# Turning the weights of the states' reads on VectorE and by transfers inside SBUF, turning all states first and all reads last, and splitting the last stores

## The chip, the cores and the metric

The kernel runs on one core of a Trainium2 chip. The metric is the device time of one execution in microseconds (us). Every kernel below was run several times, beside runs of the kernel before on the same chip, and each run comes with the mean clock that TensorE was granted.

The engines are TensorE (PE in the profile; PEld is its weight load), VectorE (DVE), ScalarE (ACT), GpSimd (POOL) and SyncE (SP). SyncE here only issues transfers.

## The reference

Eight batches of eight heads hold 512 tokens and 32 states of width 64. Tokens attend to states, and states attend to tokens. The two results stand below one another (4352 rows of 512) and go through a feed-forward of width 2048.

```python
scores  = x @ state^T / 8;   xread = softmax(scores)  @ state     # 512 rows a batch
scores2 = state @ x^T / 8;   sread = softmax(scores2) @ x         # 32 rows a batch
X = concat(xread, sread) as (8 * 544, 512)
h = X @ w_in                                                      # 512 -> 2048
g = h * erf(max(h, 0) + log1p(exp(-|h|)))
out = g @ w_out                                                   # 2048 -> 512
```

## The kernel before

The token rows of a batch never form `xread`. Their hidden layer is `softmax(scores) @ (state @ w_in)`. The product `state @ w_in` is called the mixing (tile `m`, operands `w_in,st`). It is made of small matmuls of 64 rows by 32 columns, which run side by side on TensorE. The large products (hidden: tiles `h<-`; second products: tiles `o<-`) are done on 2x2 blocks with seven products in place of eight; VectorE makes the sums that this needs. A batch has four groups of hidden and second products. While batch b is in these, the attention of batch b+1 is made beside them.

The parts that the change touches are these:

```python
def states(b):                               # once a batch
    ps = ps_at.tile([P, P], F32, name="at")
    nc.tensor.transpose(out=ps, in_=st[:, b, :], identity=ident)
    stT[b] = keep.tile([P, P], F32, name="stT")
    nc.scalar.copy(stT[b], ps)

def turn_weights(a2):                        # eight transposes, two copies a batch
    a2T = att.tile([P, 2, NC, P], F32, name="sc")
    for e in range(2):
        ps = ps_at.tile([P, NC, P], F32, name="at")
        for c in range(NC):
            nc.tensor.transpose(out=ps[:, c, :], in_=a2[:, e, P * c:P * c + P],
                                identity=ident)
        nc.scalar.copy(a2T[:, e], ps)
    return a2T

def attention(b):
    # [...] turns xq, scores, softmax of both sides
    for e in range(2):
        normalise(both[:, e].rearrange("p (k n) -> p k n", n=Ns))
        nc.vector.transpose(out=aT[b][:, e], in_=both[:, e])
    yield
    a2T = turn_weights(both[:, 2:4])
    yield
    sn = read_tokens(b, a2T, z2)             # 64 small matmuls, sread of one batch
    if b + 1 < B:
        load_x(b + 1)
    yield
    turn_read(b, sn)                         # one transpose and one copy a batch
    yield
```

The argument also rests on the second products and on the sums that they need. The sums are made on VectorE while the first of the products run on TensorE:

```python
def project7(gT, hs, g, first, last, acc):
    # [...]
    for n, (lhs, rhs, bank, c) in enumerate((
            (A12, B21, 0, 0), (A11, B11, 2, 0), (A22, T[4], 1, 0), (S2, T[2], 0, 1),
            (S3, T[3], 2, 1), (S1, T[1], 1, 1), (S4, B22, 3, 0))):
        for i in range(GF):
            if i == 2 and n == 1:
                tt(S1, A21, A22, op=ALU.add)
                tt(S2, S1, A11, op=ALU.subtract)
                tt(S3, A11, A21, op=ALU.subtract)
                tt(S4, A12, S2, op=ALU.subtract)
            nc.tensor.matmul(out=acc[bank][:, E2 * c:E2 * c + E2], lhsT=lhs[:, i, :],
                             rhs=rhs[:, g, i, :], ...)

def put_s(r, ot, c=slice(0, d_model)):       # the last stores, of the states' rows
    m = P // Ns
    rows = out.rearrange("(b t) e -> b t e", t=TB)[m * r:m * r + m, S:]
    nc.sync.dma_start(out=rows[:, :, c], in_=ot[:, c])
```

Of the kernel before, what the change touches and what calls it, by code (L numbers as in the profile page):

```python
# [16 lines left out]
def kernel(  # L17
# [128 lines left out]
    def warm(n):  # L146

        for _ in range(n):
            nc.tensor.matmul(out=spare[:, 0:P], lhsT=ident, rhs=ident, start=True, stop=True)


    sT = const.tile([P, NK, B, Ns], F32, name="sT")
    stT = {}
    aT = {}

    def states(b):

        ps = ps_at.tile([P, P], F32, name="at")
        nc.tensor.transpose(out=ps, in_=st[:, b, :], identity=ident)
        stT[b] = keep.tile([P, P], F32, name="stT")  # L160
        nc.scalar.copy(stT[b], ps)

    over = lambda t: t.unsqueeze(2).to_broadcast([P, NC * NI, Ns])

# [2 lines left out]
    def scores(b, xT):  # L167


        s2 = [ps_at.tile([P, S], F32, name="at") for _ in range(2)]  # L170
        for i in range(NI):
            for e in range(2):
                r, q = slice(D * e, D * e + D), slice(Ns * i, Ns * i + Ns)
                on_pe = nc.tensor.matmul(out=s2[e][q, :], lhsT=stT[b][r, q], rhs=xT[r, i, :],
                                         start=True, stop=True)
        sc = att.tile([P, 2, S], F32, name="sc")
        for e in range(2):
            last = nc.scalar.copy(sc[:, e], s2[e])
        marks[:] = last, on_pe
        return sc, last  # L180
# [21 lines left out]
    def turn_weights(a2):  # L202
# [6 lines left out]
            nc.scalar.copy(a2T[:, e], ps)  # L209
        return a2T  # L210

    def read_tokens(b, a2T, z2):


        xt = x_t.pop(b)
        sr = ps_at.tile([P, 2, D], F32, name="at")
        for e in range(2):
            for c in range(NC):
                for i in range(NI):
                    q = slice(Ns * i, Ns * i + Ns)  # L220
                    nc.tensor.matmul(out=sr[q, e, :], lhsT=a2T[:, e, c, q],  # L221
                                     rhs=xt[:, c, 2 * i + e, :],
                                     start=(c == 0), stop=(c == NC - 1))
        sn = small.tile([P, 2, D], F32, name="sn")
        for e in range(2):
            nc.vector.tensor_scalar(sn[:, e], sr[:, e], z2[:, e:e + 1], None, op0=ALU.mult)
        return sn

    def turn_read(b, sn):
        ps = ps_at.tile([P, NI, Ns], F32, name="at")  # L230
        nc.tensor.transpose(out=ps, in_=sn, identity=ident)
        nc.scalar.copy(sT[:, :, b, :], ps)

    def attention0(between):


        xt = x_t[0]
        xT = att.tile([P, NI, S], F32, name="xT")
        for i in range(NI):
            xp = ps_at.tile([P, S], F32, name="at")  # L240
            for c in range(NC):
                nc.tensor.transpose(out=xp[:, P * c:P * c + P], in_=xt[:, c, 2 * i:2 * i + 2, :],
                                    identity=ident)
            nc.scalar.copy(xT[:, i, :], xp)
        sc, on_act = scores(0, xT)
        both = att.tile([P, NI, S], F32, name="xT")
        a = both[:, 0:2].rearrange("p e (k n) -> p e k n", n=Ns)
        aT[0] = keep.tile([P, 2, S], F32, name="aT")
        for e in range(2):
            s1 = ps_at.tile([P, NC * NI, Ns], F32, name="at")  # L250
            for c in range(NC):
                on_pe = nc.tensor.transpose(out=s1[:, NI * c:NI * c + NI, :],
                                            in_=sc[:, e, P * c:P * c + P], identity=ident)
            m1 = small.tile([P, NC * NI], F32, name="m1")
            nc.vector.reduce_max(out=m1, in_=s1, axis=AX.X)
            on_dve = nc.vector.tensor_tensor(a[:, e], s1, over(m1), op=ALU.subtract)
        between(on_pe, on_act, on_dve)
        for e in range(2):
            on_act = nc.scalar.activation(out=a[:, e], in_=a[:, e], func=ACTF.Exp, scale=scale)
            on_dve = normalise(a[:, e])  # L260
        for e in range(2):
            ps = ps_at.tile([P, S], F32, name="at")
            for c in range(NC):
                nc.tensor.transpose(out=ps[:, P * c:P * c + P],
                                    in_=a[:, e, NI * c:NI * c + NI, :], identity=ident)
            nc.vector.tensor_copy(aT[0][:, e], ps)

        def rest():
            a2 = both[:, 2:4]
            z2 = weigh_tokens(sc, a2)  # L270
            turn_read(0, read_tokens(0, turn_weights(a2), z2))

        return rest, on_act, on_dve

    def attention(b):



        xq = xq_t.pop(b)
        xT = att.tile([P, NI, S], F32, name="xT")  # L280
        turned = nc.vector.transpose(out=xT.rearrange("p i t -> p (i t)"),
                                     in_=xq.rearrange("p i m d -> p (i m d)"))
        if b + 1 < B:
            load_xq(b + 1)
        sc, _ = scores(b, xT)
        marks.append(turned)
        yield
        both = att.tile([P, NI, S], F32, name="xT")
        aT[b] = keep.tile([P, 2, S], F32, name="aT")
        for e in range(2):  # L290
            nc.vector.transpose(out=both[:, e], in_=sc[:, e])
            a = both[:, e].rearrange("p (k n) -> p k n", n=Ns)
            m1 = small.tile([P, NC * NI], F32, name="m1")
            nc.vector.reduce_max(out=m1, in_=a, axis=AX.X)  # L294
            nc.vector.tensor_tensor(a, a, over(m1), op=ALU.subtract)  # L295
            nc.scalar.activation(out=a, in_=a, func=ACTF.Exp, scale=scale)
        z2 = weigh_tokens(sc, both[:, 2:4])
        for e in range(2):
            normalise(both[:, e].rearrange("p (k n) -> p k n", n=Ns))
            nc.vector.transpose(out=aT[b][:, e], in_=both[:, e])  # L300
        yield
        a2T = turn_weights(both[:, 2:4])
        yield
        sn = read_tokens(b, a2T, z2)
        if b + 1 < B:
            load_x(b + 1)
        yield
        turn_read(b, sn)
        yield

    m_t = {}
# [6 lines left out]
    def mixed_part(b, g, j, parts, copy):  # L318
        n = gw // parts
        mg = m_t[b, g][:, :, n * j:n * j + n]  # L320
        fs = slice(2 * g + j, 2 * g + j + 2 // parts)
        ps = [ps_at.tile([P, gw], F32, name="at")[:, 0:n] for _ in range(2)]
        for i in range(NI):
            for e in range(2):
                r, q = slice(D * e, D * e + D), slice(Ns * i, Ns * i + Ns)
                nc.tensor.matmul(out=ps[e][q, :], lhsT=stT[b][r, q],  # L326
                                 rhs=w_in[r, fs, i, :], start=True, stop=True)
        return nc.scalar.copy(mg[:, 0], ps[0]), copy(mg[:, 1], ps[1])

# [200 lines left out]

    def put_s(r, ot, c=slice(0, d_model)):
        m = P // Ns
        rows = out.rearrange("(b t) e -> b t e", t=TB)[m * r:m * r + m, S:]
        nc.sync.dma_start(out=rows[:, :, c], in_=ot[:, c])

    def tiles(n):
        return [ps_o.tile([P, d_model], F32, name="o%d" % r) for r in range(n)]
# [38 lines left out]
            mixed(b, 2 * g + j, copy=copy)  # L576
        combine_m(b, g)

    def begin(on_pe, on_act, on_dve):
        with tc.issue_after(on_pe.ins):  # L580
            warm(32)
        with tc.issue_after(on_act.ins), tc.issue_after(on_dve.ins):
            weights_in(0)

    def behind(marks, f, *args):
        with ExitStack() as order:
            for m in marks:
                order.enter_context(tc.issue_after(m.ins))
            return f(*args)



    warm(10)
    states(0)
    rest, *at = attention0(begin)
    behind(at, weights_in, 1)
    at = mixed(0, 0, 2)
# [7 lines left out]
    for g in range(1, NG):  # L605
# [20 lines left out]
            for j in range(2):  # L626
                behind(at, weights_out, 2 * g + j)
        if g == NG - 1:
            behind(fetched[-1:], load_st)
            behind(fetched[-1:], load_xq, 1)  # L630
            behind(done_, rest)
            load_x(1)
            states(1)
            turn = attention(1)
        gT_, (gT, hs, banks) = gT, hidden(0, range(GF * g, GF * g + GF))
        if g < NG - 1:
# [11 lines left out]
        if g == 2:  # L648
            done(project(gT_, g - 1, acc))
    prepare(1, 1 - begins(1), nc.scalar.copy)  # L650
    done(turn)
    last = behind(at, combine_w)

    def pending():
# [3 lines left out]
    for b in range(1, B + 1):  # L658
# [3 lines left out]
            groups = fast(b, 1, lambda h: put_s)  # L662
        for g, (first, second) in enumerate(groups):
            side = {}
            if b + 1 < B:

                if g == 0:
                    side[4] = lambda: states(b + 1)
                    turn = attention(b + 1)
                    side[6] = lambda: behind(marks, next, turn)  # L670
                elif g == 1:
                    side[0] = side[6] = side[10] = lambda: next(turn)
                else:
                    if g == 2:
                        side[2] = lambda: next(turn)
                    o = g - 2 ^ begins(b + 1)
                    side[4] = lambda: mixed(b + 1, 2 * o)
                    side[8] = lambda: (mixed(b + 1, 2 * o + 1), combine_m(b + 1, o))
                    if g == 3:
                        side[6] = lambda: combine_a(b + 1)  # L680
            elif b + 1 == B and g > 1:

                if g == 2:
# [42 lines left out]
```

## Time and profile before

| | before |
|---|---|
| time, median of 3 runs | 763.88 us (763.88 to 764.07) |
| PE busy | 741.8 us, 97% of the span |
| VectorE busy | 512.7 us, 67% |
| ScalarE busy | 386.8 us, 51% |
| one batch of 2 to 6, start to start | 82.60 us |
| last matmul's start to the end of the span | 8.64 us |

PE is the bound, and a batch is one PE queue with next to no gaps.

### The profile page before, as it was taken

Reading aid. Unit: us, or ns where it says so; the run is one execution under the profiler, and the core shown is the slowest. Engines: PE = TensorE matmul, PEld = TensorE weight load, DVE = VectorE, ACT = ScalarE, POOL = GpSimd, SP = SyncE. Lnnn points to the kernel's source line nnn. Section 1 sums busy time; section 2 is a strip of 40 time slices with the busy share of each in tenths; the row PEclk is TensorE's granted clock in tenths of the full one; section 3 lists DMA queues with packets and bytes.
Section 4 is the critical chain, followed back from the end, with each engine's and each line's share of the span. In section 5 each row is a group of like instructions: output and inputs, shape, how many; then the busy total and the mean of one; then the engine's idle time right before and its main releaser. Section 6 shows DMA issues by size and latency. Waiting matters only on the chain.

```text
span 761.9 us, 12108 instructions
## 1 busy us (share of the span) xinstructions
PE 741.8 (97%) x5076; PEld 595.8 (78%) x5076; DVE 512.7 (67%) x767; ACT 386.8 (51%) x497; POOL 0.7 (0%) x6
## 2 busy tenths in 40 slices
PE   8998999999999999999999999999999999999995
PEld 6533435698888888988888888888898889999994
DVE  3888879856767566947595776756694755684441
ACT  5868864744465544553464446554455344443330
POOL 0000000000000000000000000000000000000000
PEclk9999999999999999999999999999999999999999
DMA  7665752420031201320042003120000000000000
GB/s 225 202 244 202 165 96 70 98 57 28 1 52 43 53 22 17 68 57 28 1 83 57 28 1 51 48 48 22 1 29 2 29 1 28 1 28 1 28 1 29
DMA packets 108587, 42.74 MB, mean 56 GB/s; under 512 B 96116, under 2 KB 99956, under 8 KB 108532
## 3 DMA queue, kind: packets, MB, share of 16 engines
q1 hardware_dynamic: 106420, 41.43, 20.4%
q8 instruction: 40, 0.66, 0.3%
q10 hardware_dynamic: 2112, 0.52, 0.3%
q14 instruction: 15, 0.12, 0.1%
HBM read 33.03 MB, written 8.91 MB: 55 GB/s over the span
## 4 chain that ended last, share of the span: by engine, by line
PE 78%; DVE 10%; ACT 3%; issue 1%; DMA 0%; SPq 0%; DVEq 0%
PE o L503 44%; PE h L397 23%; PE at L326 3%; PE o L453 2%; PE h L439 2%; ACT s L447 1%; DVE hs L405 1%; DVE m L194 1%; PE at L221 1%; DVE z L184 1%; DVE raw L475 1%; DVE xT L295 1%; ACT L447 1%; DVE m L294 1%; DVE s L448 1%
## 5 line engine op out<-in xcount | busy, mean ns | idle before, releaser
L448 DVE TENSOR_TENSOR s<-s,hs 128x2048 f32<-128x2048 f32 x34 | 77.9, 2292 | 74.2 <-ACT s L447 74.1
L404 ACT ACTIVATE s<-hs 128x512 f32<-128x512 f32 x120 | 75.6, 630 | 86.2 <-DVE hs L405 85.9
L503 PE MATMUL o<-w_out,s 128*128 128x256 f32 x480 | 118.3, 380 | 0.0
L503 PE MATMUL o<-raw,hs 128*128 128x256 f32 x480 | 116.3, 385 | 0.0
L503 PE MATMUL o<-w_out,hs 128*128 128x256 f32 x480 | 115.4, 381 | 0.0
L503 PEld LDWEIGHTS o<-raw,hs 128*128 128x128 f32 x480 | 88.4, 190 | 31.4 <-issue 20.1
L503 PEld LDWEIGHTS o<-w_out,hs 128*128 128x128 f32 x480 | 89.8, 190 | 16.3 <-issue 4.2
L405 DVE TENSOR_TENSOR hs<-hs,h 128x512 f32<-128x512 f32 x90 | 61.5, 684 | 49.8 <-PE h L397 49.7
L503 PEld LDWEIGHTS o<-w_out,s 128*128 128x128 f32 x480 | 84.5, 191 | 7.8
L397 PEld LDWEIGHTS h<-aT,m 128*128 128x128 f32 x672 | 84.4, 192 | 6.4 <-issue 1.6
L397 PE MATMUL h<-aT,m 128*128 128x128 f32 x672 | 85.6, 276 | 0.4 <-DVE hs L405 0.4
L405 DVE TENSOR_TENSOR hs<-s,h 128x512 f32<-128x512 f32 x60 | 41.1, 685 | 56.2 <-PE h L397 55.8
L447 ACT ACTIVATE s<-s 128x2048 f32<-128x2048 f32 x34 | 65.0, 1911 | 0.4
L408 ACT COPY s<-h 128x512 f32<-128x512 f32 x30 | 17.5, 582 | 92.4 <-PE h L397 92.4
L453 PE MATMUL o<-w_out,s 128*128 128x512 f32 x128 | 59.1, 600 | 0.9 <-DVE s L448 0.9
L397 PE MATMUL h<-sy,sx 128*128 128x128 f32 x448 | 59.5, 275 | 0.0
L397 PEld LDWEIGHTS h<-sy,sx 128*128 128x128 f32 x448 | 56.7, 192 | 2.2 <-ACT hs L413 0.6
L503 PE MATMUL o<-raw,s 128*128 128x256 f32 x240 | 57.9, 379 | 0.0
L413 ACT COPY hs<-h 128x512 f32<-128x512 f32 x30 | 17.4, 582 | 73.7 <-PE h L397 73.7
L503 PEld LDWEIGHTS o<-raw,s 128*128 128x128 f32 x240 | 43.3, 191 | 4.6
L453 PEld LDWEIGHTS o<-w_out,s 128*128 128x128 f32 x128 | 23.1, 191 | 30.0 <-issue 28.8
L447 ACT ACT_TABLE_LOAD x34 | 43.6, 1283 | 0.6
(112 smaller groups left out, 902.7 us busy)
## 6 DMA issues: line engine op xcount, KB each, us to landing
raw<-in_moe_w_in_dram SPq DMA_DIRECT2D x8, 1024.0 KB, 5.2
raw<-in_moe_w_out_dram SPq DMA_DIRECT2D x8, 1024.0 KB, 4.9
x<-in_x_dram SPq DMA_DIRECT2D x60, 128.0 KB, 2.7
xq<-in_x_dram SPq DMA_DIRECT2D x112, 64.0 KB, 2.1
out_dram<-ot SPq DMA_DIRECT2D x19, 256.0 KB, 2.0
out_dram<-ot SPq DMA_DIRECT2D x30, 128.0 KB, 1.7
x<-in_x_dram ACTq DMA_DIRECT2D x4, 128.0 KB, 4.1
st<-in_state_dram SPq DMA_DIRECT2D x8, 56.0 KB, 4.2
```

What stands on the lines that cost most here:

```text
L184: nc.vector.reduce_sum(out=z1, in_=a, axis=AX.X)
L326: nc.tensor.matmul(out=ps[e][q, :], lhsT=stT[b][r, q], rhs=w_in[r, fs, i, :], start=True, stop=True)
L397: last = nc.tensor.matmul(out=bank[:, q], lhsT=lhsT, rhs=rhs, start=(first and i == 0 and k == 0), stop=(i == GF - 1 and k == len(ops) - 1 ...
L404: nc.scalar.activation(out=s[:, k], in_=hs[:, k], func=ACTF.Softplus)
L405: add = lambda o, x, y: nc.vector.tensor_tensor(o, x, y, op=ALU.add)
L408: nc.scalar.copy(m1, p)
L413: nc.scalar.copy(c11, p)
L439: on_pe = nc.tensor.matmul(out=hp, lhsT=m_t[b, f // GF][:, e, P * (f % GF):P * (f % GF) + P], rhs=aT[b][:, e], start=(e == 0), stop=(e == 1))
L447: return (nc.scalar.activation(out=s, in_=s, func=ACTF.Erf), nc.vector.tensor_tensor(s, s, hs, op=ALU.mult))
L448: nc.vector.tensor_tensor(s, s, hs, op=ALU.mult))
L453: nc.tensor.matmul(out=acc[r], lhsT=gT[:, i, P * r:P * r + P], rhs=w_out[:, GF * g + i, :], start=(g == 0 and i == 0), stop=(g == NG - 1 a ...
L503: nc.tensor.matmul(out=acc[bank][:, E2 * c:E2 * c + E2], lhsT=lhs[:, i, :], rhs=rhs[:, g, i, :], start=(first and i == 0 and c == 0), stop ...
```

## The change

The intent was to take 64 transposes out of PE's queue. VectorE turns the weights in 32x32 blocks, and sixteen transfers from SBUF to SBUF put the blocks in their places. All eight states are turned in the first batch, in place of four of the 32 warm-up matmuls there. All eight reads are turned together in the last batch. The last stores are split as well, so that each goes to one batch's 32 rows and two engines issue them.

```diff
-    def states(b):
+    def states(bs):
+        ps = ps_h.tile([P, len(bs), P], F32, name="h")
+        for k, b in enumerate(bs):
+            last = nc.tensor.transpose(out=ps[:, k], in_=st[:, b, :], identity=ident)
+        nc.scalar.copy(st[:, bs[0]:bs[-1] + 1, :], ps)
# [... cut]
-    def turn_read(b, sn):
+    def turn_read(bs):
+        ps = ps_at.tile([P, len(bs), NI, Ns], F32, name="at")
+        for k, b in enumerate(bs):
+            nc.tensor.transpose(out=ps[:, k], in_=sn_t[b], identity=ident)
# [... cut: attention]
-        a2T = turn_weights(both[:, 2:4])
-        yield
-        sn = read_tokens(b, a2T, z2)
+        nc.vector.transpose(out=both[:, 0:2], in_=both[:, 2:4])
+        a2T = att.tile([P, 2, NC, P], F32, name="sc")
+        blocks = both[:, 0:2].rearrange("p e (c m n) -> p m (e c) n", m=NI, n=Ns)
+        rows = a2T.rearrange("p e c (i n) -> p i (e c) n", n=Ns)
+        for m in range(NI):
+            for i in range(NI):
+                nc.sync.dma_start(out=rows[Ns * m:Ns * m + Ns, i],
+                                  in_=blocks[Ns * i:Ns * i + Ns, m])
+        yield
+        read_tokens(b, a2T, z2)              # now in the batch's own first quarter
# [... cut: put_s]
-        rows = out.rearrange("(b t) e -> b t e", t=TB)[m * r:m * r + m, S:]
-        nc.sync.dma_start(out=rows[:, :, c], in_=ot[:, c])
+        for j in range(m):
+            r0 = TB * (m * r + j) + S
+            queue = nc.scalar if r == 1 or (c.start and j % 2) else nc.sync
+            queue.dma_start(out=out[r0:r0 + Ns, c], in_=ot[Ns * j:Ns * j + Ns, c])
# [... cut: begin]
+        behind(fetched[-1:], load_st)
+        on_pe = behind([on_pe], warm, 12)
+        for bs in range(1, 5), range(5, B):
+            on_pe = behind([on_pe], states, bs)
+        return behind([on_pe], warm, 16)
```

More of the change, by code (lines that the diff above doesn't have):

```diff
@@ L148, in warm @@
         for _ in range(n):
-            nc.tensor.matmul(out=spare[:, 0:P], lhsT=ident, rhs=ident, start=True, stop=True)
+            last = nc.tensor.matmul(out=spare[:, 0:P], lhsT=ident, rhs=ident, start=True,
+                                    stop=True)
+        return last
     sT = const.tile([P, NK, B, Ns], F32, name="sT")
-    stT = {}
     aT = {}
-    def states(b):
-        ps = ps_at.tile([P, P], F32, name="at")
-        nc.tensor.transpose(out=ps, in_=st[:, b, :], identity=ident)
-        stT[b] = keep.tile([P, P], F32, name="stT")
-        nc.scalar.copy(stT[b], ps)
+    def states(bs):
[3 more added lines that the diff above has]
+        nc.scalar.copy(st[:, bs[0]:bs[-1] + 1, :], ps)
+        return last
     over = lambda t: t.unsqueeze(2).to_broadcast([P, NC * NI, Ns])
@@ L173, in scores @@
                 r, q = slice(D * e, D * e + D), slice(Ns * i, Ns * i + Ns)
-                on_pe = nc.tensor.matmul(out=s2[e][q, :], lhsT=stT[b][r, q], rhs=xT[r, i, :],
+                on_pe = nc.tensor.matmul(out=s2[e][q, :], lhsT=st[r, b, q], rhs=xT[r, i, :],
                                          start=True, stop=True)
@@ L210, in turn_weights @@
         return a2T
+    sn_t = {}
     def read_tokens(b, a2T, z2):
@@ L218, in read_tokens @@
             for c in range(NC):
-                for i in range(NI):
+                for i in reversed(range(NI)):
                     q = slice(Ns * i, Ns * i + Ns)
@@ L223, in read_tokens @@
                                      start=(c == 0), stop=(c == NC - 1))
-        sn = small.tile([P, 2, D], F32, name="sn")
+        sn = sn_t[b] = const.tile([P, 2, D], F32, name="sn0") if b == 0 else \
+            st[:, b - 1, :].rearrange("p (e d) -> p e d", e=2)
         for e in range(2):
             nc.vector.tensor_scalar(sn[:, e], sr[:, e], z2[:, e:e + 1], None, op0=ALU.mult)
-        return sn
-    def turn_read(b, sn):
-        ps = ps_at.tile([P, NI, Ns], F32, name="at")
-        nc.tensor.transpose(out=ps, in_=sn, identity=ident)
-        nc.scalar.copy(sT[:, :, b, :], ps)
+    def turn_read(bs):
+        ps = ps_at.tile([P, len(bs), NI, Ns], F32, name="at")
+        for k, b in enumerate(bs):
+            nc.tensor.transpose(out=ps[:, k], in_=sn_t[b], identity=ident)
+        nc.scalar.copy(sT[:, :, bs[0]:bs[-1] + 1, :].rearrange("p i b n -> p b i n"), ps)
     def attention0(between):
@@ L256, in attention0 @@
             on_dve = nc.vector.tensor_tensor(a[:, e], s1, over(m1), op=ALU.subtract)
-        between(on_pe, on_act, on_dve)
+        on_pe = between(on_pe, on_act, on_dve)
         for e in range(2):
@@ L263, in attention0 @@
             for c in range(NC):
-                nc.tensor.transpose(out=ps[:, P * c:P * c + P],
-                                    in_=a[:, e, NI * c:NI * c + NI, :], identity=ident)
+                with tc.issue_after(on_pe.ins):
+                    nc.tensor.transpose(out=ps[:, P * c:P * c + P],
+                                        in_=a[:, e, NI * c:NI * c + NI, :], identity=ident)
             nc.vector.tensor_copy(aT[0][:, e], ps)
@@ L270, in rest @@
             z2 = weigh_tokens(sc, a2)
-            turn_read(0, read_tokens(0, turn_weights(a2), z2))
+            read_tokens(0, turn_weights(a2), z2)
         return rest, on_act, on_dve
@@ L300, in attention @@
             nc.vector.transpose(out=aT[b][:, e], in_=both[:, e])
+        nc.vector.transpose(out=both[:, 0:2], in_=both[:, 2:4])
[6 more added lines that the diff above has]
+                                  in_=blocks[Ns * i:Ns * i + Ns, m])
         yield
-        a2T = turn_weights(both[:, 2:4])
-        yield
-        sn = read_tokens(b, a2T, z2)
+        read_tokens(b, a2T, z2)
         if b + 1 < B:
             load_x(b + 1)
-        yield
-        turn_read(b, sn)
         yield
@@ L325, in mixed_part @@
                 r, q = slice(D * e, D * e + D), slice(Ns * i, Ns * i + Ns)
-                nc.tensor.matmul(out=ps[e][q, :], lhsT=stT[b][r, q],
+                nc.tensor.matmul(out=ps[e][q, :], lhsT=st[r, b, q],
                                  rhs=w_in[r, fs, i, :], start=True, stop=True)
@@ L577, in prepare @@
         combine_m(b, g)
-    def begin(on_pe, on_act, on_dve):
-        with tc.issue_after(on_pe.ins):
-            warm(32)
-        with tc.issue_after(on_act.ins), tc.issue_after(on_dve.ins):
-            weights_in(0)
     def behind(marks, f, *args):
@@ L589, in behind, with begin @@
             return f(*args)
+    def begin(on_pe, on_act, on_dve):
+        behind([on_act, on_dve], weights_in, 0)
+        behind(fetched[-1:], load_st)
[3 more added lines that the diff above has]
+        return behind([on_pe], warm, 16)
     warm(10)
-    states(0)
+    states(range(1))
     rest, *at = attention0(begin)
@@ L628 @@
         if g == NG - 1:
-            behind(fetched[-1:], load_st)
             behind(fetched[-1:], load_xq, 1)
@@ L632 @@
             load_x(1)
-            states(1)
             turn = attention(1)
@@ L650 @@
     prepare(1, 1 - begins(1), nc.scalar.copy)
-    done(turn)
     last = behind(at, combine_w)
@@ L664 @@
             side = {}
+            if b < B and g == 0:
+                side[2] = lambda turn=turn: next(turn)
             if b + 1 < B:
                 if g == 0:
-                    side[4] = lambda: states(b + 1)
                     turn = attention(b + 1)
@@ L671 @@
                 elif g == 1:
-                    side[0] = side[6] = side[10] = lambda: next(turn)
+                    side[0] = lambda: next(turn)
                 else:
-                    if g == 2:
-                        side[2] = lambda: next(turn)
                     o = g - 2 ^ begins(b + 1)
@@ L680 @@
                         side[6] = lambda: combine_a(b + 1)
+            elif b + 1 == B and g == 1:
+                side[4] = lambda: [turn_read(range(k, min(k + 4, B))) for k in range(0, B, 4)]
             elif b + 1 == B and g > 1:
```

## The prediction

> **What bounds the kernel now.** I read the page first, then the stretches of one batch each, then the timeline inside one batch, the waits of the tensor engine, and last the end of the kernel.
>
> ```profile
> PE 741.8 (97%) x5076; PEld 595.8 (78%) x5076; DVE 512.7 (67%) x767; ACT 386.8 (51%) x497; POOL 0.7 (0%) x6
> ...
> PE 78%; DVE 10%; ACT 3%; issue 1%; DMA 0%; SPq 0%; DVEq 0%
> ```
>
> The first line is busy time by engine, the second the engines on the chain that ended last. TensorE is the bound, with VectorE on the chain for a tenth of the span. Batches 1 to 6 are alike:
>
> ```profile
> 225.52:308.12 82.60, 82.40 (x604) 70.06 (x603) 57.12 (x92) 41.61 (x55) 0.00 (x0) 1.00 0.18 41
> 308.12:390.70 82.58, 82.38 (x603) 70.06 (x602) 57.10 (x92) 41.60 (x55) 0.00 (x0) 1.00 0.17 39
> ```
>
> The columns are length, then PE, PEld, DVE, ACT, POOL busy. A batch takes 82.6 us, PE is busy in all but 0.2 of it, VectorE in 57. So PE work taken out of a batch shortens it, if VectorE, which has 25 us to spare on average, is not late where PE needs it. The timeline of PE in the second quarter of a batch, where the attention of the next batch is made:
>
> ```profile
> 236.98 0.60 PE L503 MATMUL o<-raw,s 128*128 128x256 f32 x2
> 237.41 0.38 PE L207 MATMUL at<-ident,xT 128*128 128x128 f32 x2
> 237.63 1.96 PE L503 MATMUL o<-raw,hs 128*128 128x256 f32 x8
> 239.43 0.82 PE L207 MATMUL at<-ident,xT 128*128 128x128 f32 x6
> 240.09 0.38 PE L503 MATMUL o<-w_out,hs 128*128 128x256 f32 x1
> ```
>
> The columns are start and time covered. One transpose is listed at 273 ns, but that is latency. From start to start, six take 240.09 - 239.43 = 0.66 us: 0.11 us each is what one costs the queue. VectorE in the same place:
>
> ```profile
> 235.68 0.70 DVE L300 STREAM_TRANSPOSE aT<-xT 128x512 f32<-128x512 f32 x1
> 236.30 0.65 DVE L405 TENSOR_TENSOR hs<-hs,h 128x512 f32<-128x512 f32 x1
> 236.87 0.67 DVE L500 TENSOR_TENSOR hs<-hs,s 128x512 f32<-128x512 f32 x1
> 237.47 0.68 DVE L501 TENSOR_TENSOR hs<-s 128x512 f32<-128x512 f32 x1
> ```
>
> There is no idle time between these, nor back to about 222.7: here VectorE is full. L500 makes the operand of the PE group that starts at 237.63 and is ready at 237.54. The average of 67% hides that this quarter has 0.1 us of slack. PE already waits once in it:
>
> ```profile
> PE h L397 <- DVE hs L405: 1.4, 6, 0.4
> ```
>
> That is us in total, times, longest: 0.4 us in nearly every batch, the only matmul wait listed between 142 and 630 us. The end:
>
> ```profile
> SPq L721 <- DMA out_dram<-ot: 5.7, 1, 5.7
> ...
> DMA packets 397, 0.53 MB, mean 44 GB/s; under 512 B 12, under 2 KB 268, under 8 KB 396
> ```
>
> The first line: SyncE waits 5.7 us for the last store. The second counts the packets after 750 us: only 12 small ones, the completion writes of three stores, so four engines for each store.
>
> **What the Trainium skill says.** "VectorE: DVE Perf Modes", The three transpose paths: VectorE turns 32x32 blocks only, TensorE a full 128x128 into PSUM. The code before uses both so, and the trace has 0.68 to 0.70 us for 128x512 on VectorE. "TensorE: Matmul & The Clock Gate", Part 4: PE-mode transpose, gives about 275 ns in a kernel, mostly access latency; the trace has 273 listed and 0.11 between starts, which agrees and is why I count 0.11. "DMA: Bandwidth & Descriptors", Why a DMA increments its semaphore by 16 and not by 1: the engines used are the largest number up to 16 that divides the slowest dimension of both sides. The last stores have a slowest dimension of 4 on the DRAM side; 12 completions for three stores agree. The same page, Specifications: under 512 B a transfer is not at line rate. The load of xq, in 128 B packets, shows what that means here: from 219 to 231 us its sixteen transfers of 64 KB moved at about 130 GB/s.
>
> **The change, part by part.**
>
> *Out of each steady batch on PE.* Eight transposes of the weights, one of the states, one of the read: 10 x 0.11 = 1.1 us. The wait for the copy of the turned states before the scores (weight loads at L174 waited 1.8 us in five times) is mostly under other work; the start before it is 0.1 us late. Together 1.2 us in each of six batches: 7.2 us.
>
> *Into VectorE.* One turn of 128x1024. From 0.70 us at 512 columns and 2.30 at 2048 (L281), I estimate 0.70 + 512 x 1.6/1536 = 1.23 us, in seven batches. It overwrites the half that the last L300 reads, so it falls in right after that, in the full stretch, and ahead of L500, as softmax work was issued ahead of L500 all along. L500 then ends at 237.54 + 1.23 = 238.8. PE, without its two transposes, asks at 237.41: a new wait of up to 1.4 us, more than the batch saves. If L500 is put first there is none. I cannot see which from the diff and take half, 0.65 us x 6 = 3.9 us given back. Net for the steady batches: 3.3 us.
>
> *Out of ScalarE.* Two copies of 0.57 us and two of 0.25 in each batch. ScalarE is off the bound at 42 of 82.6 us; nothing counted.
>
> *Transfers.* Sixteen of 32 KB in 128 B packets: 4096 packets a batch, half of xq's. Sixteen xq issues took 9.3 us. The read is moved to the first quarter of the next batch, some 55 us later, so the transfers are hidden. The exception is batch 1: softmax ends near 116 us, issue and landing take until about 125, and PE read the tokens at 121. There PE already stands 1.8 us before L231 at 128.5, as VectorE is late, so most of the wait replaces another.
>
> *The first batch.* Out go two read transposes with waits of 0.4 and 1.8 us, eight weight transposes (0.9) and one state. But from 104 to 129 us the chain is VectorE, which gets 1.23 more and loses 0.47 (the read's scaling moves on). At the start, two copies (about 1.0 us, est. from 0.58 for 512 columns) enter ScalarE where it is full from 12.2 to 17.8 us, and the states' load goes ahead of weights that are not needed before 15.6. The turning itself takes the place of warm-up matmuls: 12 + 7 + 16 for 32. I count 0.5 us gained in all.
>
> *The last batches.* Eight transposes appear in batch 7: 8 x 0.11 = 0.9 us lost.
>
> *The end.* The last add ends at 754.1. Each final store becomes four of 32 rows, so sixteen engines each, on two issuing queues. A 128 KB store on sixteen engines lands in 1.7 us (page, DMA issues). Two issues of some 0.36 us and 1.7 to 2 us of landing give about 756.7 instead of 754.66 + 5.7 = 760.4. I count 3.5 us gained.
>
> Sum: -3.3 - 0.5 + 0.9 - 3.5 = -6.4; 763.9 - 6.4 = 757.5 us.
>
> **The rivals.**
>
> *VectorE gives all of it back.* For it: L500 has 0.1 us of slack and a wait of 1.4 would exceed the 1.2 saved. Against: the order could be luckier, and VectorE loses the read's scaling from the next quarter. Then steady batches stay at 82.6 to 82.8, and the time is 760 to 762 us.
>
> *No wait at all, PE gets all.* For it: average load of VectorE is only 69% in a batch; the turned weights are not needed for 55 us, so a good order would put them behind L500. Then 81.4 us a batch, and 753 to 754 us.
>
> *Transfers become the wait.* If the sixteen small transfers, or the loads of x and the stores behind them on the same queue, are late, PE stands before the read in every batch. Against it: they have some 55 us, and SyncE would be issuing for about a third of a batch (9.3 us for xq, as much for these, some 8 for x and the stores). It would cost several us a batch and make the change slower, 770 or more. I give it 2%.
>
> *The start is delayed by the states' load.* ScalarE and the weights are near the path there; it would cost 1 to 3 us once.
>
> **Range and chances.** The two ends of the VectorE question are 753.6 and 762.0; the first batch and the end add about 1.5 us either way. 752.5 to 763 should hold it 8 times in 10. Two per cent faster is 748.6, which needs the full 7.2, the 3.5 and another 5 us from the first batch: 3%. Two per cent slower needs waits for transfers in all batches: 2%.
>
> **What would show it.** Starts of equal groups a batch apart: 81.4 means the whole PE gain, 82.6 means VectorE took it. A PE wait of L503 for the line of L500 (the sums of the second product) in the second quarter would be the new wait. In the end, 3 x 4 x 16 = 192 instead of 12 completion writes, and SyncE's last wait near 2 us in place of 5.7. Wrong would be: PE waiting for the transfers of the turned weights in steady batches, a first batch longer by over 2 us, or the last wait unchanged.

## More of the kernel before

The order in which an engine receives its instructions is set by the compiler's scheduler, except where the kernel says `issue_after`.

## The result, and the profile after

The changed kernel took 756.48 us (median of 4 runs, 755.29 to 757.16), and the kernel before took 763.95 beside it (763.88 to 764.07). The ratio is 0.99, with a 95% interval of 0.9883 to 0.9918. A ratio here is the mean time of one kernel's fast runs over the mean of the other's fast runs in the same rounds, so it is not quite the ratio of the medians quoted. The change is 7.5 us faster: less than 2%, but clear of noise. The predicted 757.5 was 1 us off.

The page of the changed kernel, busy time by engine and the chain that ended last:

```profile
PE 740.5 (98%) x5012; PEld 590.9 (78%) x5012; DVE 520.8 (69%) x774; ACT 381.1 (51%) x473; POOL 0.7 (0%) x6
...
PE 81%; DVE 8%; ACT 2%; issue 1%
```

PE has 64 instructions fewer, VectorE has 8 us more work, and VectorE's share of the chain has gone down, from 10% to 8%. Two steady batches, with the columns length, PE, PEld, DVE, ACT, POOL busy:

```profile
226.42:307.97 81.55, 81.48 (x594) 68.83 (x594) 58.22 (x93) 40.39 (x51) 0.00 (x0) 1.00 0.21 46
307.97:389.52 81.55, 81.48 (x595) 68.83 (x594) 58.23 (x93) 40.39 (x51) 0.00 (x0) 1.00 0.22 46
```

A batch takes 1.05 us less than before. That is nearly all of the 1.1 us that ten transposes cost PE, so nothing of it was lost to a late VectorE. The timeline of VectorE in the stretch where the prediction expected the trouble:

```profile
237.02 1.23 DVE L310 STREAM_TRANSPOSE xT<-xT 128x1024 f32<-128x1024 f32 x1
238.17 0.65 DVE L512 TENSOR_TENSOR hs<-s 128x512 f32<-128x512 f32 x1
238.74 0.68 DVE L514 TENSOR_TENSOR hs<-s 128x512 f32<-128x512 f32 x1
239.34 0.68 DVE L513 TENSOR_TENSOR hs<-hs,s 128x512 f32<-128x512 f32 x1
```

The turn takes the estimated 1.23 us. It stands where it was expected, ahead of the sums. L512 to L514 make the sums S1, S3 and S2, in this order. S2 (L513) is now ready only at 240.02. Counted from the start of its group's first hidden product that is 13.8 us, where it was 12.0 before (237.54 against 225.52): 1.75 us later, as the turn, S1 and S3 now stand just before it (S1 had been made at 222.66 before). PE in the same stretch:

```profile
236.95 1.46 PE L516 MATMUL o<-raw,s 128*128 128x256 f32 x6
238.25 1.05 PE L410 MATMUL h<-aT,m 128*128 128x128 f32 x8
239.14 0.60 PE L516 MATMUL o<-raw,hs 128*128 128x256 f32 x2
239.57 1.03 PE L516 MATMUL o<-w_out,hs 128*128 128x256 f32 x4
```

PE does not wait. Between the products that need no sum (`raw,s`) and the next ones stand eight products `h<-aT,m`, which belong to the next group. Before, they came after all the second products: the first hidden product of that group stood at 246.65, and now it stands at 238.25. The products on the sums are also in another order. The two `raw,hs` at 239.14 start before S2 is ready, so they can only be on S1 (ready at 238.82), the other sum that meets a `raw` operand. The four `w_out,hs` at 239.57 are by the same reasoning on S3 (ready at 239.42); before, S2 came first. So two things fill the hole, the eight hidden products and the products on the earlier sums. This order is the same in three profiles of the changed kernel, so it is the compiled order. Why the scheduler chose it is not recorded. The waits of PE's matmuls from 142 to 630 us (total, times, longest) are now one line, and the old wait (1.4 us in six times, 0.4 at most) is not among them:

```profile
PE o L516 <- DVE s L461: 0.2, 1, 0.2
```

The SBUF transfers, in the page's list of issues (count, size, median us from issue to landing), and then SyncE's last wait:

```profile
sc<-xT SPq DMA_DIRECT2D x112, 32.0 KB, 1.9
```

```profile
SPq L736 <- DMA out_dram<-ot: 1.6, 1, 1.6
```

No PE wait in a steady batch names the transfers. SyncE's wait for the last store is 1.6 us where it was 5.7. The packets from 742 us to the end, and the issues there:

```profile
DMA packets 576, 0.53 MB, mean 38 GB/s; under 512 B 192, under 2 KB 448, under 8 KB 576
...
out_dram<-ot SPq DMA_DIRECT2D x6, 32.0 KB, 1.6
out_dram<-ot ACTq DMA_DIRECT2D x2, 32.0 KB, 1.6
```

There are 192 small packets where there were 12, so each of the twelve stores uses sixteen engines.

Where the time went can be read from equal places in the two traces. The zero is the first hidden product of batch 0, because the start of the two profiles differs by chance (see the experiments). The changed kernel's column is its third profile, which started as the kernel before did.

| from the first hidden product, us | before | changed | difference |
|---|---|---|---|
| that product, from the span's start | 23.34 | 23.31 | 0.0 |
| batch 1 begins | 92.18 | 91.44 | -0.7 |
| batch 2 begins | 182.48 | 180.88 | -1.6 |
| batch 7 begins | 595.50 | 589.04 | -6.5 |
| states' rows begin | 668.86 | 664.50 | -4.4 |
| last matmul starts | 729.91 | 725.56 | -4.4 |
| span ends | 738.6 | 730.0 | -8.6 |

### The profile page after: what moved, and what is told of

It is laid out like the page before. It is cut to its first block, busy times and chain, and to the rows that moved or that the text cites. A ratio compares the mean times of both kernels' runs of the same rounds, so it can differ in the third digit from the quotient of the medians.

```text
span 754.5 us, 12132 instructions
## 1 busy us (share of the span) xinstructions
PE 740.5 (98%) x5012; PEld 590.9 (78%) x5012; DVE 520.8 (69%) x774; ACT 381.1 (51%) x473; POOL 0.7 (0%) x6
## 4 chain that ended last, share of the span: by engine, by line
PE 81%; DVE 8%; ACT 2%; issue 1%
PE o L516 46%; PE h L410 25%; PE at L339 4%; PE o L466 3%; PE h L452 2%; DVE hs L418 1%; PE at L226 1%; DVE m L197 1%; DVE z L187 1%; PE at L177 1%; DVE raw L488 1%; ACT s L460 1%; DVE xT L303 1%; ACT L460 1%; DVE xT L190 0%
```

## The experiments

My theory was this. Stores and batches each give about half of the gain, and the batches keep PE's whole gain only because the scheduler moved other products into the hole that VectorE's turn makes. The rival was that VectorE was never late, because it had 25 us to spare in each batch. A second question was whether the first batch loses time, at its start (the first profile of the changed kernel had its first hidden product at 24.70, 1.4 us later than before) or at its end, where VectorE is the chain.

### The new stores alone

The kernel before, with one edit:

```diff
-        rows = out.rearrange("(b t) e -> b t e", t=TB)[m * r:m * r + m, S:]
-        nc.sync.dma_start(out=rows[:, :, c], in_=ot[:, c])
+        for j in range(m):
+            r0 = TB * (m * r + j) + S
+            queue = nc.scalar if r == 1 or (c.start and j % 2) else nc.sync
+            queue.dma_start(out=out[r0:r0 + Ns, c], in_=ot[Ns * j:Ns * j + Ns, c])
```

> The kernel before with one part of the change: the last stores cut into blocks of 32 rows on two issuing queues. Theory: from the last matmul's start to the end of the span the kernel before takes 761.9 - 753.3 = 8.6 us and the changed one 754.5 - 750.1 = 4.4 us, and that is the stores alone. So 763.9 - 4.2 = 759.7 us here, with TensorE's last matmul where it was, 192 small completion packets at the end and a last wait of SyncE near 1.6 us. Rival: the gain of 7.5 us is all work taken from TensorE, and the end of the stores is not in the measured time: 763.9 us.

Its three fast runs took 761.41, 760.3 and 760.05 us, and the kernel before 763.93 (median of 7). The ratio is 0.9955 (0.9938 to 0.9971), about 3.4 us. The profiled run was slow (854.01 us at a mean clock of 0.849) and is not compared. That is the 3.5 of the prediction; this run's own expectation, read off the ends of the two profiles, was 4.2. As the profile is slow, the end in this kernel is not compared.

### Everything but the stores

The changed kernel with the old `put_s`, the reverse of the edit above.

> The changed kernel with the old last stores (one transfer for a tile). If the two parts simply add, 756.5 + 4.2 = 760.7 us, and what is left, some 3.2 us against the kernel before, is what moving the transposes earns after all its costs. Rival, the parts share something (the end only became short because TensorE ended in another way): not 760.7 but nearer 756.5.

It took 759.83 us (759.47 to 761.22), a ratio of 0.9948 (0.9933 to 0.9963), or 4.0 us. The two halves add up: 3.4 + 4.0 = 7.4, against 7.5 for the whole change. This rules out that one part covers for the other.

### The weights turned by TensorE again

```diff
# on the changed kernel
-        nc.vector.transpose(out=both[:, 0:2], in_=both[:, 2:4])
-        # [... tile and sixteen transfers]
+        yield
+        a2T = turn_weights(both[:, 2:4])
# [...]
-                    side[0] = lambda: next(turn)
+                    side[0] = side[6] = lambda: next(turn)
```

> The changed kernel, but the weights of the states' reads turned by TensorE again (eight transposes and two ScalarE copies a batch, no VectorE turn, no transfers inside SBUF); states still turned in the first batch, reads turned late, new stores. Theory: each steady batch gets its 8 x 0.11 = 0.87 us back, 81.55 becomes 82.4, and over six batches 5.2 us; the end of the first batch, where VectorE is the chain, gains up to 1.2 us. So 756.5 + 5.2 - 1 = 760.7 us. Rival, VectorE's turn and the transfers cost as much as they save: 756 to 757 us.

It took 759.45 us (758.21 to 761.56), about 3 us more than the changed kernel. In its trace a steady batch takes 82.27 us. Of the 1.05 us that a batch gained, 0.7 is the weights' turning (eight transposes) and 0.3 is the states and reads. At the beginning of batch 2 it is 0.4 us ahead of the changed kernel (180.51 against 180.88), so there VectorE's turn seems to cost more than it saves. The changed kernel's other two profiles have 180.77 and 180.95, so this is little more than the spread.

### The order of PE held as written

On the changed kernel, each second product may only be issued after the one before it, and the next group's first hidden product and the mixing only after the latest second product. No work is added or removed.

```diff
+                with ExitStack() as order:
+                    for m in pe_last:
+                        order.enter_context(tc.issue_after(m.ins))
+                    pe_last[:] = [nc.tensor.matmul(
-                nc.tensor.matmul(
# [... the same issue_after(pe_last) around product(1, p) and around the mixing]
```

> The changed kernel with TensorE's queue held to the program's order where the changed kernel departs from it: the products of the second matmul one behind the other, and the next group's first product and the mixing behind them. VectorE's work is the same. Theory: the compiler put other TensorE work where the late sum of VectorE would have been waited for, and that is why the wait of 1.4 us that I predicted is not there. Held to the order, it is: a wait of L526 for the second product's sums of 1 to 1.5 us in each of six batches, batches of 82.5 to 83 us, and 762 to 765 us. Rival: VectorE is early enough anyway and the order is no more than a by-product: 81.6 us a batch and 756.5 us.

It took 764.16 us (763.0 to 764.88), a ratio of 1.0003 (0.9986 to 1.0019). The time is back at that of the kernel before. The gain of the stores is still there (from the last matmul's start to the end of the span this kernel takes 4.4 us), so the batches now lose as much as the stores gain. Its waits from 142 to 630 us, and PE's timeline with the wait in brackets:

```profile
PE o L526 <- DVE hs L520: 8.3, 5, 1.7
```

```profile
235.64 1.46 PE L526 MATMUL o<-raw,s 128*128 128x256 f32 x6
238.76 1.99 PE L526 MATMUL o<-raw,hs 128*128 128x256 f32 x8 [1.67 <-DVE hs L520]
```

VectorE's line that makes S2 in this kernel:

```profile
238.02 0.69 DVE L520 TENSOR_TENSOR hs<-hs,s 128x512 f32<-128x512 f32 x1
```

This is the wait of the prediction: the second product on S2 waits for S2, once in each steady batch, for 1.7 us (8.3 us in 5 times). S2 is ready at 238.71, again 13.8 us after the group's first hidden product (224.93), and VectorE makes the sums in the same order as in the changed kernel. What differs is PE's order. A batch takes 83.28 us, 1.73 more than in the changed kernel and 0.68 more than in the kernel before. So the rival that VectorE was never late is out. VectorE is late by 1.7 us in each batch, and only the order of PE's queue hides it. The run holds the products on the sums and the next group's products at once, so it does not show which of the two hides how much.

### The changed kernel again

This is the same kernel, run as the yardstick for the next three.

> The changed kernel itself once more, as the yardstick for the other three of this group and for the spread. Its four runs so far lay between 755.3 and 757.2 us. Theory (the start of this kernel varies from run to run, because the moment at which TensorE gets its full clock varies): again 755 to 757.5, median near 756.5, spread of 1.5 us or more against 0.6 of the kernel before, and PE's first hidden product in the profile starts at another time than 24.7 us by some tenths or more. Rival (a property of the first profile's chip): spread under 0.6 us.

It took 756.52 us (755.18 to 756.77), and the kernel before 765.58 (763.91 to 766.16). This time the kernel before spread widely, in two levels, about 764.0 and about 765.7, and the changed kernel spread by 1.6 us, as the theory said. But its first hidden product stood at 24.75 us, nearly where it had been, so this profile does not yet show a start that varies; the third one below does.

### Batch 1's weights on TensorE

```diff
# on the changed kernel, in attention(b)
+        if b == 1:
+            yield
+            a2T = turn_weights(both[:, 2:4])
+        else:
             nc.vector.transpose(out=both[:, 0:2], in_=both[:, 2:4])
# [... and the sixteen transfers]
```

> The changed kernel, but the weights of batch 1 alone are turned on TensorE, in batch 1's second quarter's place, as before; batches 2 to 7 as changed. Theory (from 104 to 129 us VectorE is the chain, and the 1.23 us turn of batch 1 plus its transfers sit in it): the end of the first batch gains about 1.2 us, eight transposes give 0.9 back but where PE has to wait anyway, so 0.5 to 1.2 us faster than the changed kernel: 755.3 to 756. Rival (the turn of batch 1 is hidden too, as those of the later batches are): 0.9 us slower, 757.4.

It took 755.94 us (755.38 to 757.12) beside 756.52, and its ratio to the kernel before is the same (0.9881 and 0.9878): inconclusive by the times. Its trace shows a reason: in this run TensorE was at half clock twice inside the kernel, from 66.0 and from 130.8 us, 3.4 us each, which costs half of that, 1.7 us, each time. By an estimate, without these 3.4 us it would have been ahead of the changed kernel by about 1.5 us at the beginning of batch 2 (182.91 - 3.4 = 179.5, against 180.95 in the changed kernel's second profile). But the stretches may belong to the edit: all four runs of this kernel have a mean clock of 0.995 to 0.997, the five of the changed kernel beside it 0.997 to 1.0, and the second stretch begins 0.8 us after a wait of PE of 1.84 us that is 0.4 us in the changed kernel. No run tests this.

### The states loaded and turned late

```diff
# on the changed kernel
-        behind(fetched[-1:], load_st)
-        on_pe = behind([on_pe], warm, 12)
-        for bs in range(1, 5), range(5, B):
-            on_pe = behind([on_pe], states, bs)
-        return behind([on_pe], warm, 16)
+        return behind([on_pe], warm, 32)
# [... and load_st, states(bs) at the end of the first batch]
```

> The changed kernel, but the other seven states are loaded and turned late in the first batch, as before, and the start has its 32 warm-up matmuls again. Theory (the load of the states and two more copies in the full start delay the first hidden product, which stood at 24.70 us against 23.34 before): about 1 us faster than the changed kernel, 755.5, and the first hidden product near 23.5. Rival (the late start in the one profile is the variable clock start, nothing of the change): the same as the changed kernel within 0.3 us, and the first hidden product moves with the moment of full clock.

It took 755.74 us (755.1 to 756.97), 0.8 us under the changed kernel by the medians and 0.2 by the means, with the same ratio to the kernel before (0.9878): the rival. The first hidden product against the moment of full clock, over several profiles:

| kernel | full clock from, us | first hidden product, us |
|---|---|---|
| before | 4.4 | 23.34 |
| changed, three profiles | 10.5, 10.7, 5.5 | 24.70, 24.75, 23.31 |
| everything but the stores (same start as changed) | 5.9 | 23.46 |
| states late | 6.6 | 23.49 |
| turned twice (same start as changed) | 10.4 | 24.56 |
| order held, weights on TensorE, batch 1's weights on TensorE (same start as changed) | 5.3, 5.3, 4.5 | 23.53, 23.92, 23.69 |

The late start of the first profile was the clock's, which came either near 5 us or near 10.5 us, in the same kernel. (The moment is read from the spacing of the first matmuls, 0.21 us before it and 0.11 after.) My suspicion from the first comparison is dropped: the states' load costs nothing that the times show. With an early clock the new start gave 23.31 to 23.92, against 23.34 and 23.49 with the states late, so some tenths are not excluded.

### The turn done twice

```diff
-        nc.vector.transpose(out=both[:, 0:2], in_=both[:, 2:4])
+        for _ in range(2):
+            nc.vector.transpose(out=both[:, 0:2], in_=both[:, 2:4])
```

> The changed kernel with the turn of the weights on VectorE done twice (the second writes the same result again), so VectorE has 1.23 us more in each of seven batches and nothing else changes. Theory (the compiled order of PE leaves some slack behind the late VectorE sums, and VectorE has 25 us to spare in a batch): 0 to 2 us slower, 756.5 to 758.5, most of it at the end of the first batch, and steady batches of 81.5 to 81.7 us. Rival (VectorE is at its limit in the second quarter and the reordering only just hid the first turn): 1.2 us in each batch, 763 to 765, steady batches of 82.8.

It took 760.64 us (759.87 to 761.5), 4.1 us more than the changed kernel beside it. A steady batch takes 82.40 us, 0.85 more. That lies between theory and rival, and yet PE shows no wait in such a batch. What differs in PE's busy time is the mixing. Here are the busy times of PE and PEld of the mixing's line alone over one batch, first for this kernel and then for the changed kernel:

```profile
226.12:308.52 82.40, 5.39 (x64) 0.85 (x64) 1.00 0.21 45
```

```profile
226.60:308.16 81.56, 4.36 (x64) 0.72 (x64) 1.00 0.21 46
```

The same 64 small matmuls take 1.03 us more. The timeline of the kernel that turns twice:

```profile
248.75 1.04 PE L340 MATMUL at<-w_in,st 64*32 64x512 f32 x2
...
258.67 1.08 PE L340 MATMUL at<-w_in,st 64*32 64x512 f32 x14
```

The scheduler had pulled two of the sixteen side-by-side matmuls forward. Two alone take as long as all sixteen. In the whole group eight start within 0.05 us and the other eight 0.45 us later; the two that were pulled forward are not side by side, but 0.45 us apart. I took this split for the cause, and the next run tested it.

### The turn done twice, the mixing kept whole

```diff
# on the kernel that turns twice: first mixing of a group
-                    side[4] = lambda: mixed(b + 1, 2 * o)
+                    side[4] = lambda: behind(pe_last, mixed, b + 1, 2 * o)
# [... pe_last holds the latest second product]
```

In the steady batch shown, the trace has the sixteen whole again, and two of the eight `h<-sy,sx` in the place where the two stood.

> The turn on VectorE done twice, as in the run that came to 760.64 us with steady batches of 82.40, but with one thing held: in each batch of 2 to 6 the first of the sixteen mixing products (64 rows by 32 columns, which run side by side on TensorE) may not be issued ahead of the second products it was split from. In the compiled order of PE nothing else changes. In the run before, two of them stood alone for 1.04 us and the other fourteen took 1.08, where all sixteen together take 1.09. Theory (the second turn on VectorE costs no wait in a steady batch; its cost was this split of the side-by-side products): steady batches of 81.5 to 81.6, and 756.5 to 757.5 us in all. Rival (VectorE's extra 1.23 us is what costs, the split only fills the hole): steady batches stay at 82.3 to 82.4, a wait for VectorE shows, and about 760.5 us.

It took 763.64 us (760.12 to 765.13). The runs at a mean clock of 1.0 took 760.12 and 760.59; the others had 0.992 to 0.994. A steady batch takes 82.28 us. My theory fell. With the mixing whole, PE waits openly:

```profile
249.01 0.49 PE L412 MATMUL h<-sy,sx 128*128 128x128 f32 x2 [0.68 <-ACT hs L428]
249.34 1.89 PE L519 MATMUL o<-w_out,s 128*128 128x256 f32 x8
```

The split had filled a hole. The wait that is listed is that of the two hidden products, for a copy by ScalarE that ends at 248.95. My reading is that the hole would be there without them, because the next second products (`w_out,s`) need VectorE's product `s`, and that is 1.2 us later, ready at 248.90. First the changed kernel, whose PE takes up these products at 247.74, then the kernel with the mixing whole:

```profile
245.40 2.29 DVE L461 TENSOR_TENSOR s<-s,hs 128x2048 f32<-128x2048 f32 x1 [3.93 <-ACT s L460]
```

```profile
246.61 2.29 DVE L463 TENSOR_TENSOR s<-s,hs 128x2048 f32<-128x2048 f32 x1 [3.92 <-ACT s L462]
```

In the changed kernel `s` is ready at 247.69 and is used at 247.74. So the reordering hid the one turn with 0.05 us left over at this point, and a second turn costs 0.73 us a batch as a wait or 0.85 as a split. That four of the six runs have a mean clock of 0.992 to 0.994 stays unexplained. The rival of the run before was right in kind (VectorE is at its limit) and too large in size: it had said 1.2 us.

### The changed kernel a third time

> The changed kernel a third time, the yardstick for the next two on the same chip: 755.2 to 757.2 us, median near 756.5, steady batches of 81.55 us.

It took 756.43 us (755.15 to 757.36). The runs at a mean clock of 1.0 took 755.15 and 755.65, and those at 0.998 took 757.22 and 757.36.

### Batch 1's weights on TensorE and the states late: the candidate

This is the sum of the two edits above.

> Candidate that should beat both: the changed kernel with batch 1's weights turned on TensorE (in the profile of that variant, less two stretches of half clock, PE was some 1.5 us ahead of the changed kernel at the end of batch 1) and the other states loaded late as before (which was the same as the changed kernel). In its compiled order all groups of side-by-side products are whole. Theory (VectorE's turn in the first batch costs about 1.5 us net): 1 to 2 us faster than the changed kernel of the same rounds, 754.5 to 755.5. Rival (the end of the first batch waits for other things anyway): the same within 0.5 us.

It took 755.1 us (753.53 to 755.32), and the changed kernel 756.43 beside it: 1.3 us by the medians. By the means it is 1.6 us. By equal clock it is 2.1 us at 0.998 (755.02, 755.18 and 755.32 against 757.22 and 757.36), and at 1.0 it is 753.53 against 755.15 and 755.65. Against the kernel before, the ratio is 0.9866 (0.9848 to 0.9884), where the changed kernel of the same rounds has 0.9886 (0.9867 to 0.9905). The intervals overlap, so this is a small gain that the runs of equal clock and the trace support, not one that the intervals alone prove. The mean clock is a rough sorter: it does not see the start (the first profile of the changed kernel has 1.0 with full clock only from 10.5 us), and it counts the time after the last matmul (the profile of everything but the stores has 0.997, all of it lost after 753.4 us, when the last matmul had started at 749.1). The chain of work in the changed kernel's second profile, at the end of the first batch (start, us, what):

```profile
114.73 1.20 DVE aT L308 x2
115.93 0.57 DVE sx L350
116.50 1.15 DVE xT L310
117.66 0.57 DVE sx L351
```

Here VectorE is the chain for more than 20 us, and the turn of batch 1 (L310) stands in the middle of it. In the candidate this line is gone from the chain. The candidate's granted clock is in the column after PE's busy time and count, in three stretches of its trace, and its PE timeline is in the second fence. Its batch 2 begins 181.13 us after the first hidden product, 179.4 without the half-clock stretch, as was estimated from the run of the one edit:

```profile
60.00:64.00 4.00, 2.15 (x18) 1.00 0.74 222
64.00:68.00 4.00, 3.79 (x5) 0.57 0.10 40
68.00:72.00 4.00, 4.00 (x10) 1.00 0.28 53
```

```profile
64.20 5.40 PE L456 MATMUL h<-aT,m 128*128 128x512 f32 x8 [2.04 <-ACT m L345]
```

PE waited 2.04 us for the mixing's copy, and then the clock was halved for about 3.4 us, once. This fits the levels in the run times, as a run with one more such stretch would take 1.7 us more; only the profiled run of each kernel shows its stretches. The changed kernel has the same wait, and its three profiles show no such stretch.

## Why the prediction was right or wrong

**The time** was right (756.48 for 757.5), by errors that cancel in part. That it came out so close is partly luck: the prediction took the middle between two cases that it could not tell apart.

**Steady batches: the step that failed.** "I cannot see which from the diff and take half, 0.65 us x 6 = 3.9 us given back." Nothing was given back: a batch went from 82.60 to 81.55. The premises held in the main. The turn took 1.23 us, stood ahead of the sum S2, and S2 was late, by 1.75 us rather than 1.23, as the sums S1 and S3 also moved to the place just before it. With the order held, the wait was 1.7 us in place of the predicted "up to 1.4 us", and it took more than the batches' gain (83.28 us a batch). What the prediction missed is that the order of PE's queue is not given by the program: in the compiled order other ready products stand in the hole, and the products on S1 and S3 come before those on S2. Its old wait, "0.4 us in nearly every batch", was misread too: 1.4 us in six times is 0.23 on average. The rival "no wait at all" described the result (81.4 a batch) but for another reason, the turn put behind the sum, which did not happen.

**The saving of ten transposes** was 1.05 us for 1.2. With the weights alone turned back it is 0.7 for eight, where the prediction had 8 x 0.11 = 0.9.

**First and last batches.** The prediction had -0.5 and +0.9. Up to the beginning of batch 2 the trace shows -1.6, of which the prediction's steady sum already holds one batch. In batch 7 it shows +2.1. In that sum a thing was left out: the read moved "to the first quarter of the next batch" leaves the first batch and arrives in the last. Its 64 matmuls take 1.10 us, a gain at one end and a loss at the other. The turn on VectorE at the end of the first batch then cost about 1.5 us, net of eight transposes of PE's work; this is the estimate from the runs without it. The prediction had named that chain, but it still counted a gain in all.

**The start** ("it would cost 1 to 3 us once") cost nothing that the times show; the profile that seemed to show it had a late clock.

**The transfers** were hidden, as predicted: 1.9 us from issue to landing, and no wait for them in steady batches.

**The end** was right: 3.5 predicted, 3.4 measured alone, and in the profiles the time from the last matmul's start to the end fell from 8.64 to 4.42 us, 4.2. The 192 small packets and a last wait under 2 us were both there.

**The sum by the traces** is: -0.7 to the beginning of batch 1, -0.9 in batch 1, -4.9 in batches 2 to 6, +2.1 in batch 7, and -4.2 at the end: -8.6. The medians say 7.5, as the runs differ by clock.

What stays open is why the clock is halved after a wait of 2 us in some runs and not in others, whether turning batch 1's weights on TensorE makes this more frequent, and why the full clock comes at 5 or at 10.5 us.

## What to carry to other kernels

Before counting a new wait, ask whether the waiting engine has other ready work and who sets its order: a compiled order hid 1.7 us here, but only up to 0.05 us of slack, and the next 1.23 us on the same engine cost 0.7 to 0.85 a batch. A moved piece of work leaves one end of the program and arrives at the other; count both ends. And when a difference is under 2 us, sort the runs by granted clock before believing a median, and look in the trace where the clock was lost: lost in the tail of the last stores it costs nothing, and a late start does not show in the mean.

## What the Trainium skill lacked or had wrong

- "TensorE: Matmul & The Clock Gate", Part 1: The HAM clock gate, has the clock halved after at least one idle window of about 3.4 us. Here it was halved for 3.4 us, beginning 0.3 to 1.4 us after waits of only 2.04 and 1.84 us, each time costing 1.7 us, in some runs only. It has the warm-up's end vary by about 0.5 us from run to run; here full clock came between 4.2 and 10.7 us in kernels with much the same start, and at 5.5 or 10.7 us in one kernel.
- The same page, Part 3: Packing small matmuls, gives the span of a packed group, but not what a split costs: sixteen matmuls of 64x32, in two rounds of eight that start 0.45 us apart, took 1.09 us together, and 1.04 + 1.08 us as two and fourteen.
- The same page, Part 4: PE-mode transpose, gives a duration of about 275 ns and no cost in a full queue: f32 transposes start 0.11 us apart here, and eight a batch cost 0.7 us net, 0.09 us each.
- No page says that the compiler's order of a queue may hide or make a wait. With the order held as written, the same work took 764.16 us in place of 756.48.
